# Linear attention and a gated block on one core: operands spaced apart in SBUF, sums of squares by tokens, paired stores, another order of the products

## The chip, the cores and the metric

The kernel runs on one core of a Trainium2 chip. The metric is the time of one execution on the device in microseconds (us); of several runs the median counts. One execution of the kernel before was recorded by the profiler. TensorE is called PE here (its weight loads PEld), VectorE DVE, ScalarE ACT, GpSimd POOL and SyncE SP; SBUF is the memory on the core that the engines read, PSUM the banks that PE writes.

## What is computed

```python
def phi(x):
    proj = np.einsum('bhsd,df->bhsf', x, w_phi)
    proj = proj - np.max(np.abs(proj), axis=-1, keepdims=True)
    return np.concatenate([np.exp(proj), np.exp(-proj)], axis=-1)
q_p, k_p = phi(q), phi(k)
kv, z = np.einsum('bhsf,bhsd->bhfd', k_p, v), np.sum(k_p, axis=2)
attn = np.einsum('bhsf,bhfd->bhsd', q_p, kv) / (np.einsum('bhsf,bhf->bhs', q_p, z)[..., None] + 1e-06)
x = attn.transpose(0, 2, 1, 3).reshape(B * S, H * D)
xn = x / np.sqrt(np.mean(x * x, axis=-1, keepdims=True) + 1e-06) * rms_g
g = xn @ w_gate
out = (g / (1.0 + np.exp(-g)) * (xn @ w_val)) @ w_out
```

All is float32: 8 batches of 8 heads, 576 positions, head size 64, 128 features; then x is 4608 x 512, the gate and the value weights are 512 x 1536, the output weights 1536 x 512.

## The kernel before

A float32 operand of a large product is split into a high and a low part of the type fp32r, and three matmuls (high with high, high with low, low with high) take the place of one. Nearly every matmul has 128x128 weights (the second operand named in a row of the trace) and 256 columns that stream through them (the moving operand, named first). The work goes through four stages, which overlap at their seams.

**Attention** (to about 480 us) runs over 32 pairs of heads (`front`, `mid`, `back`, `last`); lines 339 to 341 are the projections, line 443 the products with kv, the results go to the DRAM tile `xs`, transposed (channels by tokens).

**Fills** (`fill`, line 488) make 3 of the 12 column blocks of gate and value straight: for each of 18 blocks of 256 tokens, 6 units of 12 matmuls (line 503). Six blocks and a half run among the attention's work, 11 and a half behind it, until 608 us. A block is fetched from `xs` on ACT's queue (`load_x`), cast to the high part by ACT and subtracted to the low part by POOL (`_split`, lines 60 and 61), multiplied; ACT copies each unit's 128x256 result from PSUM to a tile `fo` (line 506; six buffers), and one DMA each stores it in `gvs` (line 507; ACT's queue in this stage). While the attention runs a unit takes one of the two PSUM buffers `fp`, and after it one of the three buffers `sm`. With the block's first unit pair goes `total` (line 169): the sums of squares over channels, from two fp32r matmuls with a 128x128 matrix of ones as weights' partner; ACT casts the high part (`sl`, one buffer, the low part by POOL), copies the 128x256 result and stores one row of it in DRAM (`ssd`). `invert` fetches several blocks of them, takes the root and the reciprocal, and stores the result (`rid`), from where `fetch_ri` spreads it over 128 partitions. The x operands of the fills are laid out by `apart`: the first of four channel chunks lies by itself, and the other three 48 floats (192 bytes) further on.

**Gate and value** (608 to about 1060 us) make the other 9 column blocks by a 2x2 scheme with seven products in place of eight, over 9 batches of 512 tokens. A `Group` (line 747) holds two column blocks, or one in the case of `(8,)`; a product is 6 matmuls for each column block (line 763). Products 1, 6, 7 and 4 of a group share one PSUM tile `r1`, each adding to what stands there: after 1 and after 6 ACT copies it (lines 771 and 780), after 7 and after 4 DVE adds or multiplies it in (lines 787, 790). So 6 waits for the copy of 1, 7 for the copy of 6, and 4 for the addition of 7. Products 5 and 3 share `r5` in the same way; Silu follows 3. The order of the products is written out in the loop from line 830: `run(1)` of a group, `run(7)` of the group before, then 5, 2, `run(4)` of the group before, 6, 3. A scheduler with a timeline of its own then merges it with the rest. The x operands of the next batch (`operands_x`, tiles `xo`) are made meanwhile. The results of all 12 column blocks go to the DRAM tile `hs`. In the last batch the groups run in the order `LAST`, and the output weights are fetched (`fetch_o`), combined and split (`split_o`) between groups, two of the six `kp` pieces at a time; the last two pieces, `wh4`/`wl4` and `wh5`/`wl5`, are split behind the last group.

**Output** (to the end) makes 18 groups of 256 tokens, seven products of 18 matmuls each (line 992, `omm`): operands a11, a12, s4, a22, s1, s2, s3 from one load of `hs` (`hload`, SP's queue, two buffers `ht`), split by ACT and POOL one group ahead; here the split weights `wh`, `wl` are the moving operand.

Where the SBUF tiles lie follows from the order of the pools and the sizes in them. Worked out from the program, the moving operand and the weights of a matmul lie at addresses whose difference, modulo 256 bytes, is 0 in all 3402 matmuls of line 763 and all 2268 of line 992; in the fills it is 0 for the first chunk (a quarter of line 503) and 192 for the other three; in the projections 64, and in line 443 either 0 or 128.

```python
nc.tensor.matmul(fp[:, 0:TF], w, at(xx[x], c), start=(i == 0), stop=(i == 3 * NC - 1))      # 503
nc.tensor.matmul(self.r[r][:, k], w[:, cs], x[:, h, c], start=(first and k == 0 and i == 0), # 763
nc.tensor.matmul(place[n], a[:, kp], w[:, o], start=(first and kp == 0 and i == 0),          # 992
LAST = [(8,), (0, 1), (2, 3), (4, 5), (6, 7)]                                                # 825
```

Of the kernel before, what the change touches and what calls it, by code (L numbers as in the profile page):

```python
# [82 lines left out]
def kernel(ctx: ExitStack, tc: tile.TileContext, q, k, v, w_phi,  # L83
# [20 lines left out]
    RW = 5  # L104
# [7 lines left out]
    ssd = dram.tile([1, N], F32, name="ssd")  # L112
# [10 lines left out]
    x_ctx = ExitStack()  # L123
    wfp = x_ctx.enter_context(tc.tile_pool(name="wfp", bufs=1))
# [14 lines left out]
    ones = gl.tile([128, 128], F32R, name="ones")  # L139
    nc.vector.tensor_copy(ones, one.broadcast_to([128, 128]))  # L140
# [9 lines left out]
    def apart(pool, name, n):  # L150
        t = pool.tile([128, 2, NC * n + 64], F32R, name=name)
        return [(t[:, i, 0:n].rearrange("p (c n) -> p c n", c=1), t[:, i, n + 48:n + 48 + (NC - 1) * n].rearrange("p (c n) -> p c n", c=NC - 1))
                for i in range(2)]

    def at(x, c):
        return x[1][:, c - 1] if c else x[0][:, 0]
# [12 lines left out]
    def total(bk, s2, fp, o):  # L169
# [5 lines left out]
    def invert(b0, b1):  # L175
        n = (b1 - b0) * TF // 128
        r = gl.tile([128, n], F32, name=f"inv{b0}")
        cs = slice(b0 * TF, b1 * TF)
        nc.sync.dma_start(out=r, in_=ssd[0, cs].rearrange("(p n) -> p n", p=128))
        nc.scalar.activation(r, r, AF.Sqrt, scale=1.0 / DM, bias=eps)  # L180
        nc.vector.reciprocal(r, r)
        nc.sync.dma_start(out=rid[0, cs].rearrange("(p n) -> p n", p=128), in_=r)
# [31 lines left out]
    a_ctx = ExitStack()  # L214
    xfp = a_ctx.enter_context(tc.tile_pool(name="a_xf", bufs=2))
# [3 lines left out]
    wk = a_ctx.enter_context(tc.tile_pool(name="a_wk", bufs=2))  # L219
    const = a_ctx.enter_context(tc.tile_pool(name="a_const", bufs=1))  # L220
    big = a_ctx.enter_context(tc.tile_pool(name="a_big", bufs=2))
# [6 lines left out]

    ident = const.tile([128, 128], F32, name="ident")
    make_identity(nc, ident)  # L230
# [257 lines left out]
    def fill(bk, xr):  # L488
        xx = dict(zip("hl", apart(xfp, "xo", TF)))
        with late():  # L490
            for k, x in zip(range(2), (xr[:, 0:1], xr[:, 1:NC])):
                _split(nc, xx["h"][k], xx["l"][k], x)
        with late():
            s2 = squares(xr)

        def unit(j, wi):
            js = slice(j * 128, (j + 1) * 128)
            fp = ps_s.tile([128, 512], F32, name="sm") if ended else ps_f.tile([128, T], F32, name="fp")
            i = 0
            for c in range(NC):  # L500
                a, al = wf1[wi][0][:, c, js], wf1[wi][1][:, c, js]
                for w, x in ((a, "h"), (a, "l"), (al, "h")):
                    nc.tensor.matmul(fp[:, 0:TF], w, at(xx[x], c), start=(i == 0), stop=(i == 3 * NC - 1))  # L503
                    i += 1
            o = xfp.tile([128, TF], F32, name="fo", bufs=6)
            nc.scalar.copy(o, fp[:, 0:TF])
            (nc.scalar if tail else nc.sync).dma_start(out=gvv[j][:, wi, bk * TF:(bk + 1) * TF], in_=o)
            if j == 0 and wi:
                fp = ps_s.tile([128, 512], F32, name="sm") if ended else ps_f.tile([128, T], F32, name="fp")
# [555 lines left out]
```

## Time and profile before

| | us |
|---|---|
| median of 3 runs | 1335.52 |
| lowest and highest of them | 1332.21 to 1337.31 |
| the profiled execution, its own time | 1331.64 |
| its span in the profile | 1329.9 |

In that span PE is busy for 1261.0 us (95%), DVE for 976.7 (73%), ACT for 766.3 (58%), POOL for 745.2 (56%); PE runs 10,362 instructions. In the chain of work that ended last PE has 41% of the span, DVE 8% and DMA 6%. A matmul of PE counts as busy until its modelled end, and matmuls overlap: a row with one of them shows 0.28 us, a row of six 0.88, so that five of them take 0.60. The pace is what each further matmul adds. A row of the timeline begins with the start in us and the duration in us; behind the operation stand out and in (moving operand, then weights), partitions, elements and type, and the count; in brackets the idle time ahead of it, and what ended it.

### The profile page before, as it was taken

To read this page: it belongs to the slowest core of one execution; us is meant where nothing else is said; L and a number is where in the kernel's file an instruction comes from. 1 tells how busy PE (TensorE), PEld (TensorE's weight loads), DVE (VectorE), ACT (ScalarE), POOL (GpSimd) and SP (SyncE) were. 2 spreads that over 40 slices of the span, in tenths; PEclk is the share of its full clock that TensorE was granted. 3 is DMA by queue.
4 is the path that set the end of the run, shared out by engine and by line. 5 is a ranking of instruction groups with operands and counts; after the bars stand their busy time and mean duration, and the time that the engine had idled before them with its cause. 6 is when DMAs were issued, how large, how long until landed. Compare 5 with 4: busy or idle time off the path is not lost.

```text
span 1329.9 us, 27502 instructions
## 1 busy us (share of the span) xinstructions
PE 1261.0 (95%) x10362; PEld 1243.1 (93%) x10362; DVE 976.7 (73%) x1410; ACT 766.3 (58%) x1631; POOL 745.2 (56%) x678
## 2 busy tenths in 40 slices
PE   7989999999999987989899999999999699999999
PEld 7989999999999987889899899999999699999998
DVE  6998997988787634654577778786557798877673
ACT  6988888888888755654344444443344333434332
POOL 4766665766655553772334534443332578867773
PEclk9999999999999998999999999999999699999999
DMA  5555666666665245643445554554344445444431
GB/s 160 133 149 160 176 163 171 165 183 190 169 170 148 77 134 161 199 139 108 136 159 175 162 167 159 191 155 158 121 143 136 142 147 155 128 150 153 142 128 49
DMA packets 195209, 199.77 MB, mean 150 GB/s; under 512 B 69042, under 2 KB 148804, under 8 KB 195076
## 3 DMA queue, kind: packets, MB, share of 16 engines
q1 hardware_dynamic: 175184, 179.11, 45.4%
q10 hardware_dynamic: 19892, 18.90, 4.5%
q8 instruction: 82, 1.34, 0.4%
q14 instruction: 51, 0.42, 0.1%
HBM read 128.42 MB, written 69.54 MB: 149 GB/s over the span
## 4 chain that ended last, share of the span: by engine, by line
PE 41%; DVE 8%; DMA 6%; issue 2%; ACT 2%; POOL 1%; ACTq 0%; SPq 0%; DVEq 0%; POOLq 0%
PE r L763 19%; PE gy L992 6%; PE gz L992 6%; PE gd L992 5%; PE fp L992 3%; DMA gvr<-gvs 2%; PE sm L503 2%; DMA x<-xs 1%; DVE x L191 1%; DMA hs<-gvr 1%; DVE gvr L738 1%; DVE wl L61 1%; DMA ht<-hs 1%; DVE stg L55 1%; DVE c L791 1%
## 5 line engine op out<-in xcount | busy, mean ns | idle before, releaser
L763 PE MATMUL r<-xo,wh 128*128 128x256 f32 x1764 | 326.5, 285 | 15.0 <-DVE c L787 8.8
L763 PEld LDWEIGHTS r<-xo,wh 128*128 128x128 f32 x1764 | 276.6, 193 | 18.1 <-DVE c L787 10.1
L408 POOL TENSOR_TENSOR ql<-eq,qh 128x256 fp32r<-128x256 f32 x256 | 216.9, 878 | 59.9 <-ACT qh L404 37.3
L763 PE MATMUL r<-xo,wl 128*128 128x256 f32 x882 | 246.1, 284 | 0.0
L763 PEld LDWEIGHTS r<-xo,wl 128*128 128x128 f32 x882 | 168.9, 193 | 0.0
L343 DVE TENSOR_REDUCE mx<-pp 128x4 f32<-128x512 f32 (+1 forms) x160 | 100.3, 631 | 41.3 <-PE pp L341 40.2
L379 PE MATMUL acc<-vm,ek 128*128 128x65 f32 x1024 | 129.6, 267 | 0.0
L379 PEld LDWEIGHTS acc<-vm,ek 128*128 128x128 f32 x1024 | 126.1, 192 | 0.0
L404 ACT ACTIVATE qh<-sm 128x512 fp32r<-128x512 f32 (+1 forms) x192 | 97.6, 509 | 0.0
L61 POOL TENSOR_TENSOR xo<-x,xo 128x512 fp32r<-128x512 f32 x45 | 65.4, 1463 | 47.9 <-ACT xo L60 47.7
L339 PE MATMUL pp<-wh,th 128*128 128x256 f32 x288 | 88.2, 308 | 2.6 <-DVE yk L346 1.2
L403 ACT ACTIVATE eq<-sm 128x512 f32<-128x512 f32 x128 | 78.7, 615 | 18.8 <-PE sm L392 18.0
L341 PE MATMUL pp<-wh,tl 128*128 128x256 f32 x288 | 84.2, 299 | 0.9 <-DVE tl L61 0.9
L340 PE MATMUL pp<-wl,th 128*128 128x256 f32 x288 | 81.5, 284 | 0.0
L366 ACT ACTIVATE ek<-yk 128x512 f32<-128x512 f32 x128 | 75.6, 654 | 2.4 <-DVE yk L346 2.2
L784 ACT ACTIVATE c<-c 128x1024 f32<-128x1024 f32 (+1 forms) x45 | 43.9, 976 | 53.1 <-DVE c L783 53.1
L780 ACT COPY c<-r 128x512 f32<-128x512 f32 (+1 forms) x45 | 24.4, 543 | 78.8 <-PE r L763 78.7
L61 POOL TENSOR_TENSOR s2l<-st,s2h 128x768 fp32r<-128x768 f32 x18 | 36.6, 2033 | 59.2 <-ACT s2h L60 59.2
L410 POOL TENSOR_TENSOR ql<-eqr,qh 128x256 fp32r<-128x256 f32 x32 | 24.8, 775 | 78.9 <-ACT qh L404 78.9
L54 POOL TENSOR_TENSOR wa<-raw,wa 128x192 f32<-128x192 f32 x64 | 40.8, 658 | 34.6 <-DVE wa L52 18.5
L61 DVE TENSOR_TENSOR tl<-sm,th 128x512 fp32r<-128x512 f32 (+1 forms) x96 | 50.6, 540 | 12.5 <-ACT th L60 12.4
L339 PEld LDWEIGHTS pp<-wh,th 128*128 128x128 f32 x288 | 55.3, 192 | 4.7 <-issue 2.2
(248 smaller groups left out, 4155.9 us busy)
## 6 DMA issues: line engine op xcount, KB each, us to landing
ht<-hs SPq DMA_DIRECT2D x18, 1536.0 KB
hs<-c SPq DMA_DIRECT2D x36, 512.0 KB
gvr<-gvs SPq DMA_DIRECT2D x27, 512.0 KB
rc<-di SPq DMA_DIRECT2D x32, 288.0 KB
x<-xs ACTq DMA_DIRECT2D x18, 512.0 KB
x<-xs SPq DMA_DIRECT2D x9, 1024.0 KB
gvs<-fo ACTq DMA_DIRECT2D x70, 128.0 KB
kt<-in_k_dram SPq DMA_DIRECT2D x32, 256.0 KB
```

The source lines that it names most:

```text
L61: (lo_eng or nc.vector).tensor_tensor(lo, x, hi.bitcast(F32), ALU.subtract)
L339: nc.tensor.matmul(o, th[:, cs], wh, start=True, stop=False)
L340: nc.tensor.matmul(o, th[:, cs], wl, start=False, stop=False)
L341: nc.tensor.matmul(o, tl[:, cs], wh, start=False, stop=True)
L343: nc.vector.tensor_reduce(mx[:, 0:2 * m], pp[:, 0:2 * m], axis=AX.X, op=ALU.max, apply_absolute_value=True)
L366: nc.scalar.activation(e[h][:, sg], y["k", h], AF.Exp, scale=1.0 - 2.0 * sg)
L379: nc.tensor.matmul(acc[:, sg, h], e[h][:, sg, j], vm[:, h, j], start=False, stop=(h == 1 and j == T0 - 1))
L403: nc.scalar.activation(ei[:, sg], yi, AF.Exp, scale=1.0 - 2.0 * sg)
L404: nc.scalar.activation(hi[:, sg], yi, AF.Exp, scale=1.0 - 2.0 * sg)
L408: nc.gpsimd.tensor_tensor(lo[:, sg, cs], ei[:, sg, cs], hi[:, sg, cs].bitcast(F32), ALU.subtract)
L763: nc.tensor.matmul(self.r[r][:, k], w[:, cs], x[:, h, c], start=(first and k == 0 and i == 0), stop=(i == 3 * NP1 - 1), skip_group_check=True)
L992: nc.tensor.matmul(place[n], a[:, kp], w[:, o], start=(first and kp == 0 and i == 0), stop=(kp == KP - 1 and i == 2), skip_group_check=True)
```

## The change

- Pads (`LPAD`, `FPAD`, `GPAD`, `OPAD`, `CPAD`, `BPAD`: unused tiles of 8 to 48 floats) shift the tiles behind them. Worked out as above, the difference modulo 256 bytes is 192 in all matmuls of gate, output and fill (lines 767, 999 and 497 of the new kernel) and in the projections, and 64 or 192 in the products with kv. `apart` is gone: the x operands of a fill are one tile, cast by one instruction in place of two.
- Sums of squares: the low and high parts are gone. `total` takes the squares themselves as weights, in two plain float32 matmuls with one column of ones each, so that the sums land by tokens, 128 partitions x 2; ACT copies those into the SBUF tile `sums`. `invert` works there, transposes the result by PE and DVE, and stores it. `ssd` and its DMAs are gone; `sl` has two buffers.
- Stores: gate and value of a column block share a tile `fo`, and one DMA stores both: 54 in place of 108. After the attention the units take `sm` and `fp` in turn (`bank`), five PSUM buffers in place of three.
- Order: product 7 of a group is written behind 3 of the same group. `LAST` begins with `(0, 1)` and ends with `(8,), (6, 7)`; `last_o` fetches, combines and splits output weights from the first group on. The first `ht` is fetched by two DMAs of half the size from ACT's queue.

```diff
@@ squares, total, invert
-        s2 = xm.tile([128, 2, TF], F32R, name="sl", bufs=1)
-        nc.gpsimd.tensor_tensor(ss[:, 0:TF], ss[:, 0:TF], ss[:, TF:T], ALU.add)
-        _split(nc, s2[:, 0], s2[:, 1], ss[:, 0:TF], lo_eng=nc.gpsimd)
+        s2 = xm.tile([128, TF], F32, name="sl", bufs=2)
+        nc.gpsimd.tensor_tensor(s2, ss[:, 0:TF], ss[:, TF:T], ALU.add)
...
-        for i in range(2):
-            nc.tensor.matmul(fp, ones, s2[:, i], start=(i == 0), stop=(i == 1))
-        nc.scalar.copy(o, fp)
-        nc.scalar.dma_start(out=ssd[:, bk * TF:(bk + 1) * TF], in_=o[0:1])
+        for i in range(TF // 128):
+            nc.tensor.matmul(fp[:, i:i + 1], s2[:, i * 128:(i + 1) * 128], one, start=True, stop=True)
+        n = TF // 128
+        nc.scalar.copy(sums[:, bk * n:(bk + 1) * n], fp[:, 0:n])
@@ fill
-        xx = dict(zip("hl", apart(xfp, "xo", TF)))
+        xx = dict(zip("hl", (xfp.tile([128, NC, TF], F32R, name="xo" + n) for n in "hl")))
...
-            fp = ps_s.tile([128, 512], F32, name="sm") if ended else ps_f.tile([128, T], F32, name="fp")
+            fp = bank()
...
-            o = xfp.tile([128, TF], F32, name="fo", bufs=6)
-            nc.scalar.copy(o, fp[:, 0:TF])
-            (nc.scalar if tail else nc.sync).dma_start(out=gvv[j][:, wi, bk * TF:(bk + 1) * TF], in_=o)
+            if not wi:
+                o[j] = xfp.tile([128, 2, TF], F32, name="fo", bufs=3)
+            nc.scalar.copy(o[j][:, wi], fp[:, 0:TF])
+            if wi:
+                (nc.scalar if tail else nc.sync).dma_start(out=gvv[j][:, :, bk * TF:(bk + 1) * TF], in_=o[j])
@@ the gate loop
-    LAST = [(8,), (0, 1), (2, 3), (4, 5), (6, 7)]
+    LAST = [(0, 1), (2, 3), (4, 5), (8,), (6, 7)]
...
-            if prev:
-                prev.run(7)
             gr.run(5)
...
-            if last and n == 0:
-                wot = [fetch_o(0), fetch_o(1)]
-            if last and n > 1:
...
+            if last:
+                last_o(n)
...
+            gr.run(7)
             prev = gr
@@ hload
-        nc.sync.dma_start(out=h, in_=hsv[:, :, gi * 256:(gi + 1) * 256])
+        if gi == 0:
+            for r in range(2):
+                nc.scalar.dma_start(out=h[:, r::2], in_=hsv[:, r::2, 0:256])
+        else:
+            nc.sync.dma_start(out=h, in_=hsv[:, :, gi * 256:(gi + 1) * 256])
```

How instructions stand one behind another on an engine shows at three places. The first is ACT in the fill stage, around one block: `sl` are the squares that are split, `fo` the results of units, `x` a block as fetched, `xo` its operands. Before:

```order
L506 COPY fo_8351<-sm_8338 128x256
L60 CAST sl_8331<-ss_8329 128x256
L507 DMA gvs_58<-fo_8351 128x256
L60 CAST xo_8453<-x_8440 128x256
L60 CAST xo_8453<-x_8440 128x768
L163 ACTIVATE sq_8459<-x_8440 128x512
L506 COPY fo_8367<-sm_8354 128x256
L163 ACTIVATE ss_8458<-x_8440 128x512
L172 COPY fo_8371<-sm_8370 128x256
L506 COPY fo_8389<-sm_8376 128x256
L507 DMA gvs_58<-fo_8367 128x256
```

In the kernel after, at a like place (`xoh` is the high part of `xo`):

```order
L501 COPY fo_8409<-fp_8396 128x256
L155 ACTIVATE ss_8591<-x_8574 128x512
L155 ACTIVATE sq_8592<-x_8574 128x512
L501 COPY fo_8409<-sm_8411 128x256
L501 COPY fo_8439<-fp_8426 128x256
L503 DMA gvs_58<-fo_8409 128x2x256
L501 COPY fo_8439<-sm_8441 128x256
L60 CAST xoh_8587<-x_8574 128x1024
L503 DMA gvs_58<-fo_8439 128x2x256
```

The cast of `sl` and the store behind each copy are gone; one store stands behind two copies, which come from `sm` and `fp` in turn.

The second is PE around the sums of one block, among fill matmuls (`fg`, `fv` are fill weights, `one` the column of ones). Before:

```order
L503 MATMUL sm_9010<-xo_8980,fv1_79 128x256
L171 MATMUL sm_9026<-sl_8987,ones_93 128x256
L763 MATMUL r2_9526<-xo2_8977,wl3_8220 128x256
L171 MATMUL sm_9026<-sl_8987,ones_93 128x256
L503 MATMUL sm_9032<-xo_8980,fg0_76 128x256 x2
L503 MATMUL sm_9032<-xo_8980,fg1_77 128x256
```

After:

```order
L497 MATMUL sm_8731<-xoh_8705,fv1_79 128x256
L497 MATMUL sm_8731<-xoh_8705,fv0_78 128x256
L497 MATMUL sm_8731<-xol_8706,fv0_78 128x256
L497 MATMUL sm_8731<-xoh_8705,fv1_79 128x256
L163 MATMUL fp_8746<-one_86,sl_8714 128x1 x2
L497 MATMUL sm_8750<-xoh_8705,fg0_76 128x256
L497 MATMUL sm_8750<-xol_8706,fg0_76 128x256
```

Two matmuls of 256 columns have become two of one column each, whose weights are the squares.

The third is ACT behind the last products of the gate stage: `r1` is the PSUM tile of products 1, 6, 7 and 4, `wh4` and `wh5` the last two pieces of the output weights, `ht` the first load for the output stage, `a11h` and `s3h` its operands. Before:

```order
L771 COPY c1_14093<-r1_14095 128x2x256
L784 ACTIVATE c1_13975<-c1_13975 128x1024
L60 CAST wh3_8219<-x_13934 128x1024
L780 COPY c1_14093<-r1_14095 128x2x256
L60 CAST wh4_8221<-stg0_8231 128x768
L784 ACTIVATE c1_14093<-c1_14093 128x1024
L60 CAST wh4_8221<-stg1_8232 128x1024
L60 CAST wh5_8223<-x_14056 128x768
L60 CAST wh5_8223<-x_14056 128x1024
L60 CAST a11h_14267<-ht_14263 128x768
```

After:

```order
L775 COPY c1_13946<-r1_13948 128x2x256
L784 COPY c1_13946<-r1_13948 128x2x256
L60 CAST wh4_8128<-stg1_8139 128x1024
L788 ACTIVATE c1_13946<-c1_13946 128x1024
L60 CAST wh5_8130<-x_13821 128x768
L968 DMA ht_14094<-hs_59 128x6x256 x2
L60 CAST wh5_8130<-x_13821 128x1024
L60 CAST a11h_14099<-ht_14094 128x768
L60 CAST a12h_14103<-ht_14094 128x768
L60 CAST s3h_14116<-st_14107 128x768
```

Of the four casts behind the last copy two, those of `wh5`, stand behind Silu now, and the loads of `ht`, which ACT now issues itself, stand between them.

## Rows read from the trace of the kernel before

**Rows 1.** Stages: window, length, busy PE, PEld, DVE, ACT, POOL (instructions), granted clock, DMA, GB/s.

```profile
480.00:608.00 128.00, 108.80 (x875) 104.55 (x874) 59.00 (x72) 68.43 (x161) 65.44 (x50) 0.97 0.53 164
608.00:1010.00 402.00, 390.36 (x3208) 387.14 (x3208) 286.25 (x414) 176.96 (x318) 163.46 (x142) 1.00 0.47 152
1010.00:1060.00 50.00, 36.44 (x240) 34.71 (x239) 37.51 (x46) 22.53 (x31) 19.40 (x9) 0.76 0.51 162
1060.00:1330.00 270.00, 265.02 (x2206) 264.61 (x2205) 200.47 (x174) 101.18 (x134) 192.55 (x88) 1.00 0.42 129
```

**Rows 2.** PE and PEld busy in line 763, in 992, in 992 mid-stage; clock, DMA, GB/s.

```profile
0.00:1330.00 1330.00, 418.39 (x3402) 413.85 (x3402) 0.99 0.50 150
0.00:1330.00 1330.00, 276.92 (x2268) 275.69 (x2268) 0.99 0.50 150
1100.00:1300.00 200.00, 200.00 (x1669) 200.00 (x1669) 1.00 0.45 138
```

**Rows 3.** Timeline of PE in the gate stage: start, us, what, count.

```profile
641.22 0.88 PE L763 MATMUL r<-xo,fg 128*128 128x256 f32 x6
641.94 0.88 PE L763 MATMUL r<-xo,fv 128*128 128x256 f32 x6
```

**Rows 4.** Timeline of PE in the fill stage.

```profile
565.43 0.85 PE L503 MATMUL sm<-xo,fg 128*128 128x256 f32 x6
566.34 1.54 PE L503 MATMUL sm<-xo,fv 128*128 128x256 f32 x12
```

**Rows 5.** Timeline of PE, a fill among attention work.

```profile
360.19 0.87 PE L503 MATMUL fp<-xo,fv 128*128 128x256 f32 x6
```

**Rows 6.** Timeline of PE in attention, products of lines 339 to 341 and 443.

```profile
361.73 0.28 PE L339 MATMUL pp<-wh,th 128*128 128x256 f32 x1
...
362.08 0.29 PE L443 MATMUL sm<-qh,kv1h 128*65 128x288 f32 x1
...
363.39 0.29 PE L443 MATMUL sm<-ql,kv1h 128*65 128x288 f32 x1
```

**Rows 7.** Timeline of PE, a plain f32 product (two records) and the next two.

```profile
363.65 0.39 PE L374 MATMUL acc<-vr,er 128*128 128x130 f32 x2
363.79 0.36 PE L339 MATMUL pp<-wh,th 128*128 128x256 f32 x1
363.99 0.28 PE L340 MATMUL pp<-wl,th 128*128 128x256 f32 x1
```

**Rows 8.** Waits of PE in the fill stage, 480 to 608: us, count, longest.

```profile
PE sm L503 <- ACT fo L506: 6.0, 6, 1.7
PE sm L503 <- ACT xo L60: 4.2, 1, 4.2
```

**Rows 9.** Timeline of ACT, and below it the chain, in the fill stage.

```profile
508.25 0.41 ACT L60 CAST sl<-ss 128x256 fp32r<-128x256 f32 x1 [1.81 <-POOL ss L165]
...
532.35 5.82 DMA x<-xs
```

**Rows 10.** Waits of PE, 608 to 1010 us, and a group of ACT instructions.

```profile
PE r L763 <- DVE c L790: 6.0, 6, 1.4
PE r L763 <- DVE c L787: 5.0, 4, 2.4
...
L780 ACT COPY c<-r 128x512 f32<-128x512 f32 x36 | 21.1, 585 | 65.9 <-PE r L763 65.9
```

**Rows 11.** End of the gate stage: waits of PE, chain, window.

```profile
PE fp L992 <- ACT a11h L60: 5.5, 2, 4.7
PE r L763 <- DVE c L787: 3.8, 2, 3.7
...
1017.33 5.53 DMA x<-wos
...
1036.37 7.52 DMA ht<-hs
...
1044.00:1052.00 8.00, 4.58 (x18) 3.99 (x18) 3.65 (x4) 1.03 (x2) 2.28 (x1) 0.50 0.67 224
```

More of the change, by code (lines that the diff above doesn't have):

```diff
@@ L111 @@
     wos = dram.tile([128, KP, 4, DH], F32, name="wos")
-    ssd = dram.tile([1, N], F32, name="ssd")
     rid = dram.tile([1, N], F32, name="rid")
@@ L123 @@
     x_ctx = ExitStack()
+    gl.tile([128, LPAD], F32, name="lpad")
     wfp = x_ctx.enter_context(tc.tile_pool(name="wfp", bufs=1))
@@ L138 @@
     nc.scalar.activation(warm, one, AF.Exp)
-    ones = gl.tile([128, 128], F32R, name="ones")
-    nc.vector.tensor_copy(ones, one.broadcast_to([128, 128]))
+    ident = gl.tile([128, 128], F32, name="ident")
+    make_identity(nc, ident)
+    sums = gl.tile([128, N // 128], F32, name="sums")
     held = []
@@ L148, in fetch @@
         return x
[L150 to L156, printed above, removed]
     def squares(x):
@@ L214 @@
     a_ctx = ExitStack()
+    a_ctx.enter_context(tc.tile_pool(name="fpad", bufs=1)).tile([128, FPAD], F32, name="fpad")
     xfp = a_ctx.enter_context(tc.tile_pool(name="a_xf", bufs=2))
@@ L502, in unit, with bank @@
                 for w, x in ((a, "h"), (a, "l"), (al, "h")):
-                    nc.tensor.matmul(fp[:, 0:TF], w, at(xx[x], c), start=(i == 0), stop=(i == 3 * NC - 1))
+                    nc.tensor.matmul(fp[:, 0:TF], w, xx[x][:, c], start=(i == 0), stop=(i == 3 * NC - 1))
                     i += 1
-            o = xfp.tile([128, TF], F32, name="fo", bufs=6)
-            nc.scalar.copy(o, fp[:, 0:TF])
-            (nc.scalar if tail else nc.sync).dma_start(out=gvv[j][:, wi, bk * TF:(bk + 1) * TF], in_=o)
+            if not wi:
[3 more added lines that the diff above has]
+                (nc.scalar if tail else nc.sync).dma_start(out=gvv[j][:, :, bk * TF:(bk + 1) * TF], in_=o[j])
             if j == 0 and wi:
-                fp = ps_s.tile([128, 512], F32, name="sm") if ended else ps_f.tile([128, T], F32, name="fp")
-                total(bk, s2, fp[:, 0:TF], xfp.tile([128, TF], F32, name="fo", bufs=6))
+                total(bk, s2, bank())
                 summed.append(bk)
         return [lambda j=j, wi=wi: unit(j, wi) for j in range(J1) for wi in range(2)]
+    banks = [0]
+    def bank():
+        banks[0] += 1
+        if ended and banks[0] % 2:
+            return ps_s.tile([128, 512], F32, name="sm")
+        return ps_f.tile([128, T], F32, name="fp")
     PR = B * NP
@@ L592 @@
     stg = [wtp.tile([128, 1024], F32, name=f"stg{i}") for i in range(2)]
+    g_ctx.enter_context(tc.tile_pool(name="gpad", bufs=1, side="right")).tile([128, GPAD], F32, name="gpad")
     xops = [g_ctx.enter_context(tc.tile_pool(name="xop0", bufs=1, reuse_waits="tile", side="right"))]
@@ L823, with last_o @@
     GROUPS = [(0, 1), (2, 3), (4, 5), (6, 7), (8,)]
-    LAST = [(8,), (0, 1), (2, 3), (4, 5), (6, 7)]
+    LAST = [(0, 1), (2, 3), (4, 5), (8,), (6, 7)]
+    def last_o(n):
+        nonlocal wot
+        if 0 < n <= KP // 2:
+            with late():
+                for o in wot:
+                    combine_o(*o)
+            with late():
+                for o in wot:
+                    split_o(*o)
+        wot = [fetch_o(kp) for kp in (2 * n, 2 * n + 1) if kp < KP]
     assert not todo
@@ L849 @@
                 prev.run(4)
-            if last and n == 0:
-                wot = [fetch_o(0), fetch_o(1)]
-            if last and n > 1:
-                with late():
-                    for o in wot:
-                        split_o(*o)
-                    wot = [fetch_o(kp) for kp in (2 * n - 2, 2 * n - 1) if kp < KP]
-                    for o in wot:
-                        combine_o(*o)
+            if last:
+                last_o(n)
             gr.run(6)
@@ L885 @@
                 decs.pop(0)()
-            if last and n == 1:
-                with late():
-                    for o in wot:
-                        combine_o(*o)
         if not last:
             xb, ri = xbn, rin
-    prev.run(7)
     prev.run(4)
@@ L901, in left @@
         return ctx.enter_context(tc.tile_pool(name=name, bufs=bufs, reuse_waits="tile"))
+    left("opad").tile([128, OPAD], F32, name="opad")
     ohps = [left("ohp1"), left("ohp0")][::-1]
```

28 lines of the change are left out of this document (15 added, 13 removed).

## The prediction

> **What bounds the kernel now.** I read the table of stages first [rows 1]: in the gate stage (608 to 1010 us) PE is busy for 390.4 of 402 us, in the output stage (1060 to 1330) for 265.0 of 270. DVE reaches at most 74% there, POOL 71%, ACT 44%, the DMAs 47%. In these 672 us the time is the number of matmuls by the pace of one, and a faster helper is worth little. The two other stretches are different: behind the attention (480 to 608) PE idles for 19.2 of 128 us, at the seam (1010 to 1060) for 13.6 of 50, with the granted clock down to a mean of 0.76.
>
> So the second look is at the pace. Two groups of six gate matmuls start 0.72 us apart: 120 ns each [rows 3]. In the output stage 1669 fill 200 us: 119.8 [rows 2]. Matmuls of the same shape and types in the fill stage go faster: a row of six lasts 0.85 us, a row of twelve 1.54, and a single one 0.28 [rows 6], so each further one takes (0.85 - 0.28) / 5 = 114 or (1.54 - 0.28) / 11 = 114.5 ns [rows 4]. The clock does not explain it: it was 1.00 in the slower stage and 0.97 in the faster one [rows 1]. Nor does the name of the weights: rows 3 and 4 both have `fg` and `fv` there. What differs by the program is where the moving operand lies against the weights: 0 mod 256 bytes in gate and output, 192 in three chunks of four in the fills. The evidence is not clean, since the same fill among the attention's work goes at (0.87 - 0.28) / 5 = 118 [rows 5], and three projections, at 64, take 0.35 us or 117 each [rows 6]. I take spacing as the cause, and 118 as a second pace that a stretch may fall into.
>
> The third look is at the waits, named below where a part touches them.
>
> **The change part by part**, against the profiled execution's 1331.6 us.
>
> A. *Pace of gate and output.* All 3402 + 2268 = 5670 matmuls [rows 2] move from 0 to 192. At the fills' 114 ns: 5670 x 6 = 34 us. Not all of it arrives: waits for ACT, DVE and DMA don't shrink, and a PE that is ahead meets them sooner; the gate stage has 11.6 us of them [rows 1], of which I let a quarter grow back, 3 us. **-31**. Ends: at 117.5, between the slower rows of 192 and of 64 [rows 5, 6], 5670 x 2.5 = 14; at 113.5, which the rounding of the row of twelve allows [rows 4], 36. Below that nothing in the trace goes with 256 columns.
>
> B. *Fill matmuls and sums.* A quarter of the 1296 fill matmuls moves from 0 to 192: 324 x 6 ns = -2. The sums lose 36 matmuls at some 118 ns, 4.2 us, and gain 36 plain float32 products. The trace has one such product: its two records take 0.14 us, and the matmul behind the next starts 0.20 us later where 0.12 is usual [rows 7]. Ends: 36 x 0.14 = 5.0, or +0.8; with the slow successor as well, 36 x 0.22 = 7.9, or +3.7, and somewhat more if a one-column product waits for its weights. I take +2, and **0** for B.
>
> C. *Attention.* The 864 projections move from 64 to 192, the 768 products with kv from 0 or 128 to 64 or 192. These take (363.39 - 362.08) / 10 = 131 ns for 288 columns [rows 6]; at the fills' pace 288 / 256 x 114 = 128. That is 864 x 3 + 768 x 3 ns = 5 us if PE alone set this stage. **-3**, ends -5 and 0.
>
> D. *Waits of the fill stage.* PE waits six times for a copy `fo` by ACT, 6.0 us, at most 1.7 each, and once 4.2 us for the cast `xo` [rows 8]. ACT works in order: the cast of `sl` stood 1.81 us for POOL's sum [rows 9], and the copies that free PSUM stand behind it. The change takes that cast away, halves the stores that ACT issues, and adds two PSUM buffers, two units of 12 x 0.114 = 1.4 us, more than the longest of these waits. So I take all of the 6.0 and, since a fetch can still be late, half of the 4.2: **-8**. What is late next is the block's own cycle: a fetch of 5.8 us [rows 9], a cast of 1024 and two squares of 512 floats at the 585 ns per 512 of a copy [rows 10], some 8.2 us, against 72 x 0.114 + 0.45 for sums and seams = 8.7 on PE (the 0.45 an estimate from rows 7). That is nearly even, so the ends are wide: 0 if the fetches set the stage, -19 if all idle time goes. One thing speaks against it: gate matmuls stood between fills before and filled some gaps; now the first of them follows the last fill.
>
> E. *The seam.* [...] The weights now come a group earlier, and two casts fewer stand ahead of a11h. On the other hand products 6, 7 and 4 of the last group follow each other with nothing between, so 7 waits for ACT's copy and 4 for DVE's addition, about 2.5 us; and ACT issues the loads of `ht` only behind Silu and a cast, while the second load goes out on SP without waiting and shares the DMAs with them. SP is spared the first load, and ACT's two casts behind it wait for no one else. Ends -6 (half of what the seam loses) and +6 (a load that takes half as long again, 4 us, and what a slower clock adds). **0**.
>
> F. *Order in the gate stage.* Product 7 now follows 3 of its own group. Waits for the additions of 7 and 4 were 5.0 and 6.0 us in 402 [rows 10]; the new order has a wait for the copy in place of some. Ends -6 and +10; **0**. The fetches and combining of output weights start a group earlier on SP, DVE and POOL, which have room [rows 1].
>
> Sum: -31 + 0 - 3 - 8 + 0 + 0 = **-42**: 1289.6 for the profiled execution. That lay 3.9 us below the median of the runs, 1335.5, by which it would be 1293.5. I take 1291.
>
> [...] By rows 3 and 4 equal matmuls differ by 6 ns. [...]
>
> **The rivals.**
>
> *The slower pace at 192.* Gate and output settle at 117.5 ns as the fill among attention did [rows 5]: A is -14 less the same 3 or so, B and C are near 0, D stays. 1331.6 - 13 - 8 = about 1310 (1308 without the reserve). For it: rows 5 and 6. Against: the two rows of the fill stage, whose neighbours, like those of the gate stage, are matmuls of 256 columns.
>
> *Spacing changes nothing.* The fills may be faster by something else, such as shorter runs. Then A and C are 0, D stays: 1331.6 - 8, about 1322 with a little more for sums and order. This is also the case in which the change doesn't do what it says. Against: rows of six in both stages, 0.88 against 0.85 [rows 3, 4].
>
> *Slower: product 7 waits for ACT in every group.* 7 adds to the tile that ACT copies after 6. With nothing but product 3 between, the cover is 12 x 0.12 = 1.44 us, or 0.72 for `(8,)`. The last matmul's tail of 0.28 and the copy of 0.585 [rows 10] fit in; a Silu of 1024 floats on ACT ahead of it (some 1.1 us, estimated from two such copies) doesn't, by 0.5 us, nor does (8,)'s. If that happens in all 45 groups, 36 x 0.5 + 9 x 1.2 = 29 us are lost; at the worst, 45 x 1.35 = 61. It decides from about 1 us per group, where it eats all 42: the time would be 1350. Against: the copy of 6 stands ahead of the Silu of its own group, and ACT is busy for 44% there [rows 1].
>
> *Everything comes in.* 113.5 ns, a fill stage with hardly a gap (-15) and a seam that gains 6: 1331.6 - 36 - 3 - 15 - 6 = about 1270.
>
> **How the numbers follow.** The forecast has 0.67, the slower pace 0.15, no effect of spacing 0.08, slower 0.03, everything 0.07. From the ends of the forecast's own terms (A 14 to 36, D 0 to 19, E and F some 6 each, not all at one end) its own range is about 1277 to 1305. Range: to keep no more than 2 in 10 outside I reach to the slower pace and to the good end, **1272 to 1309**. Half a per cent is 6.7 us, about what a measurement of this kernel can tell from no change: faster by more than that 0.93 (all but the third rival and half of the second), within it 0.04, slower by more 0.03.
>
> **What would show it.** Right: rows of six gate matmuls of 0.85 us, 200 us of output work with some 1750 matmuls in place of 1669, a fill stage without waits for `fo` over 1 us, and PE idle there well under 19 us. Wrong: rows of six still at 0.88; waits of gate matmuls for the copy of line 784 (new numbering) with a count near 45; a wait for a11h of over 8 us or a longer stretch at 0.50; a fill stage as long as before, waiting for `x`.

## The result and the profile after

| | before | changed |
|---|---|---|
| median of the runs, us | 1334.83 (4 runs) | 1321.56 (4 runs) |
| lowest and highest | 1332.21 to 1337.31 | 1318.34 to 1323.44 |
| span of the record | 1329.9 | 1321.6 |

The ratio is 0.990, with an interval of 0.987 to 0.993: the kernel gains 1.0%, 13 us, where 1291 (44 us off the median then known) had been forecast. The time lies outside the stated range, above its upper end of 1309.

The pace came in. The page of windows (window, length, busy PE with its count, PEld, clock, DMA, GB/s), first all matmuls of gate (line 767) and output (line 999), then the output's in 200 us, to set beside [rows 2]:

```profile
0.00:1321.00 1321.00, 403.48 (x3402) 399.38 (x3402) 0.98 0.50 151
0.00:1321.00 1321.00, 263.12 (x2268) 261.67 (x2268) 0.98 0.50 151
1100.00:1300.00 200.00, 200.00 (x1767) 200.00 (x1766) 1.00 0.47 145
```

In 200 us stand 1767 matmuls, 113.2 ns each, where 1669 stood before (119.8). The gate has this pace too, in some stretches; in others it runs at another one. Gate matmuls of the changed kernel in two windows without a wait:

```profile
716.00:736.00 20.00, 20.00 (x179) 20.00 (x178) 1.00 0.52 172
...
910.00:940.00 30.00, 30.00 (x257) 30.00 (x256) 1.00 0.39 132
```

That is 112 and 117 ns, at the same addresses (a short window also counts matmuls that only reach into it). By the starts of all matmuls between the 378th and the 3024th of the gate (seven of its nine batches), 1320 follow at 113 or 114 ns and 1098 at 115 to 118, here called 117 (140 more at 119).

Where the gain went shows in the table by stage (columns as in [rows 1]):

```profile
480.00:608.00 128.00, 109.47 (x872) 105.90 (x871) 54.77 (x67) 65.05 (x146) 61.68 (x45) 0.95 0.53 163
608.00:1010.00 402.00, 383.06 (x3245) 380.35 (x3244) 266.52 (x403) 173.19 (x317) 162.77 (x141) 0.98 0.46 150
1010.00:1060.00 50.00, 32.79 (x242) 30.62 (x241) 38.77 (x58) 24.83 (x34) 21.02 (x8) 0.85 0.58 190
1060.00:1321.00 261.00, 256.86 (x2244) 255.99 (x2243) 200.98 (x176) 97.26 (x136) 195.55 (x89) 1.00 0.43 134
```

In the gate stage PE is idle for 18.9 us of 402 (11.6 before), and its mean clock is 0.98 in place of 1.00. The same windows hold nearly the same number of matmuls as before: 3245 against 3208. Two marks and the end cut the span: the last start in the row of products with kv that is shown, and the first start of an output matmul. The page of single lines, of before and of after (name, count, least, median and largest ns, first and last start):

```profile
L443 PE MATMUL sm<-qh,kv0h x80: 290/294/378, 187.1 to 471.7; 128*65 128x288 f32 x80
...
L992 PE MATMUL fp<-wh,a11h x108: 279/283/580, 1045.1 to 1313.2; 128*128 128x256 f32 x108
```

```profile
L437 PE MATMUL sm<-qh,kv0h x80: 289/293/380, 191.0 to 477.6; 128*65 128x288 f32 x80
...
L999 PE MATMUL fp<-wh,a11h x108: 276/276/579, 1052.2 to 1305.6; 128*128 128x256 f32 x108
```

| part of the span | before | after | difference | forecast |
|---|---|---|---|---|
| attention, to the first mark | 471.7 | 477.6 | +5.9 | -3 |
| fills, gate, seam, to the second | 573.4 | 574.6 | +1.2 | -25 |
| output, to the end | 284.8 | 269.4 | -15.4 | -14 |

(The forecast's 31 us for gate and output are shared out by count: 2268 x 6 ns for the output, the rest, with the 8 us of the fill stage, to the middle.) The output stage did what was forecast. The middle, where 25 us should have gone, gained nothing, and the attention lost 6. The two records lie 8.3 us apart and the medians 13.3; the record of the changed kernel is of the slowest of its four runs, 1323.44.

What PE waited for in the gate stage (608 to 1010 us: total, times, longest), for [rows 10]:

```profile
PE r L767 <- DVE c L794: 13.8, 6, 4.0
PE r L767 <- DVE c L781: 3.2, 3, 1.7
PE r L767 <- ACT c L775: 1.5, 1, 1.5
```

Line 794 is DVE's multiplication behind product 4 (790 before), which sets free the tile `r1`. The longest of the six, on PE, on DVE ahead of it, and on SP:

```profile
704.93 1.65 PE L767 MATMUL r<-xo,fv 128*128 128x256 f32 x6 [3.98 <-DVE c L794]
```

```profile
701.66 1.23 DVE L742 TENSOR_TENSOR gvr<-gvr,ri 128x1024 f32<-128x1024 f32 x1 [3.07 <-DMA gvr<-gvs]
...
703.00 0.68 DVE L787 TENSOR_TENSOR c<-c,r 128x512 f32<-128x512 f32 x1
703.60 0.68 DVE L744 TENSOR_TENSOR gvr<-gvr 128x512 f32<-128x512 f32 x1
704.20 0.68 DVE L794 TENSOR_TENSOR c<-c,r 128x512 f32<-128x512 f32 x1
```

```profile
693.93 0.38 SPq L745 DMA_DIRECT2D hs<-gvr  x1
694.36 0.42 SPq L261 DMA_DIRECT2D wos<-stg  x1
697.95 0.37 SPq L738 DMA_DIRECT2D gvr<-gvs  x1
```

`gvr` has one buffer. The product of gate and value leaves it for `hs` at 693.9; the next load, ahead of which SP waited 3.1 us for that store, is issued at 698.0 and lands at 701.7. DVE, whose rows follow the program's order, stands at line 742 until then; the multiplication of line 794 is queued behind it, and PE behind that. Of the six waits for line 794, four (11.6 of the 13.8 us) follow such a stand of DVE at line 742; the other two stand behind other work of DVE. Then PE runs at half the clock for a while, by the windows around it:

```profile
690.00:704.00 14.00, 10.95 (x97) 10.75 (x95) 9.30 (x14) 6.01 (x12) 3.83 (x6) 1.00 0.39 126
704.00:712.00 8.00, 7.07 (x37) 7.07 (x38) 6.72 (x11) 2.34 (x6) 5.71 (x6) 0.57 0.71 243
712.00:740.00 28.00, 28.00 (x249) 28.00 (x248) 17.62 (x30) 12.01 (x23) 10.20 (x10) 1.00 0.47 156
```

37 matmuls in the 7.1 us from 704.9 on, most of them at half the clock (0.50 from 705 to 710 us, 0.57 on the mean of the window), and 249 in the next 28. At 113 ns the 37 would have taken 4.2 us, so the wait of 4.0 us cost some 7.

### The profile page after: what moved, and what is told of

It reads as the page before. It is cut to its first block, busy times and chain, and to the rows that moved or that the text cites. A ratio compares the mean times of both kernels' runs of the same rounds, so it can differ in the third digit from the quotient of the medians.

```text
span 1321.6 us, 27396 instructions
## 1 busy us (share of the span) xinstructions
PE 1242.5 (94%) x10401; PEld 1223.8 (93%) x10401; DVE 951.3 (72%) x1394; ACT 747.3 (57%) x1595; POOL 731.9 (55%) x660
## 5 line engine op out<-in xcount | busy, mean ns | idle before, releaser
L767 PE MATMUL r<-xo,wh 128*128 128x256 f32 x1764 | 312.2, 280 | 7.9 <-DVE c L794 4.1
L767 PEld LDWEIGHTS r<-xo,wh 128*128 128x128 f32 x1764 | 268.9, 190 | 10.1 <-DVE c L794 4.7
L767 PE MATMUL r<-xo,wl 128*128 128x256 f32 x882 | 242.1, 279 | 0.0
L61 POOL TENSOR_TENSOR xo<-x,xo 128x512 fp32r<-128x512 f32 x45 | 60.7, 1355 | 41.5 <-ACT xo L60 41.5
L497 PE MATMUL fp<-xoh,fg 128*128 128x256 f32 x336 | 72.9, 293 | 5.1 <-ACT xoh L60 3.7
L61 POOL TENSOR_TENSOR s2l<-st,s2h 128x768 fp32r<-128x768 f32 x18 | 42.3, 2352 | 49.5 <-ACT s2h L60 42.9
L497 PE MATMUL fp<-xoh,fv 128*128 128x256 f32 x320 | 65.9, 285 | 3.9 <-ACT fo L501 3.3
L54 POOL TENSOR_TENSOR stg<-stg,stg 128x128 f32<-128x128 f32 x48 | 23.8, 518 | 80.7 <-DVE stg L52 48.3
L767 PE MATMUL r<-xo,fv 128*128 128x256 f32 x324 | 49.7, 287 | 16.5 <-DVE c L794 12.4
L61 POOL TENSOR_TENSOR wl<-stg,wh 128x1024 fp32r<-128x1024 f32 x10 | 24.5, 2452 | 72.5 <-ACT wh L60 72.5
```

The lines of the kernel that those rows point to most:

```text
L61: (lo_eng or nc.vector).tensor_tensor(lo, x, hi.bitcast(F32), ALU.subtract)
L497: nc.tensor.matmul(fp[:, 0:TF], w, xx[x][:, c], start=(i == 0), stop=(i == 3 * NC - 1))
```

## The experiments

Theory 1: the pace is set by the distance, and in the gate stage the round trip of `gvr` through DMA takes its gain back. Theory 2: the new order of the products makes the waits. Times of experiments are medians; each experiment ran beside the kernel before on the same chip. What is said of stages comes from one record of each.

**The spacing alone.** The kernel before with pads, so that gate, fill and output are at 192 (which also makes the operands of a fill one tile, cast by one instruction, as in the changed kernel):

```diff
+    FPAD, GPAD, OPAD = 48, 16, 16
...
-        xx = dict(zip("hl", apart(xfp, "xo", TF)))
+        xx = dict(zip("hl", (xfp.tile([128, NC, TF], F32R, name="xo" + n) for n in "hl")))
+    g_ctx.enter_context(tc.tile_pool(name="gpad", bufs=1, side="right")).tile([128, GPAD], F32, name="gpad")
+    left("opad").tile([128, OPAD], F32, name="opad")
```

> The kernel before with nothing but unused tiles that put the moving operand 192 bytes (mod 256) from the weights in all gate, fill and output matmuls; order, sums, stores and loads as before. Theory 1 (the pace of one matmul comes in as forecast, 120 to 113-115 ns, and in the gate stage a fixed round trip through DMA, the load of gvr that stands in DVE's order ahead of the additions PE waits for, takes most of it back): output stage 266 us in place of 281, gate stage shorter by only 5 to 12, whole about 1310. Theory 2 (the round trip is harmless, the new order of the products made the waits): with the old order the gate stage gains its full 20 us too, whole about 1297. If spacing were not the cause of the pace: 1335.

Measured: 1320.6 against 1335.3, ratio 0.990 (0.987 to 0.993). So the pads alone give as much as the whole change; the rest of it, taken together, gave nothing (which hides a loss and a gain, see the old order below). In the output 1767 matmuls stand in 200 us, as in the changed kernel. In the gate stage the pace was there, at its faster value:

```profile
900.00:980.00 80.00, 80.00 (x706) 80.00 (x707) 1.00 0.44 144
```

113.3 ns; and yet the matmuls 378 to 3024 of the gate took 321.3 us (before: 327.2), since waits of over 0.28 us rose from 8.0 to 14.5 and matmuls at half clock from 15 to 52. Theory 2 alone, with 1297, falls: the old order loses the gain as well. The measured time is some 10 us above theory 1 too: from the end of the attention to the 378th gate matmul the record has 185.9 us, 178.2 before. Why is open.

**Everything but the spacing of gate and output.** The changed kernel without `gpad` and `opad`.

> The changed kernel without the two pads of gate and output, so that these 5670 matmuls are at 0 mod 256 again. Theory 1: output stage 281 again (+15.5), gate matmuls at 120 ns but fewer waits, gate stage longer by 5 to 10; whole 1342 to 1347, above the kernel before. Theory 2: the waits stay, since the order makes them, and gate and output lose all of it: +35, about 1356.

Measured: 1339.4, ratio 1.0031 (1.0018 to 1.0044); the output has 1669 matmuls in 200 us again. The change without these two pads costs 4 us, and the two pads are worth 18 here. Theory 1 is the nearer one, though 1339 lies below its 1342; theory 2's 35 us is refuted.

**The load of gvr set free.** In the changed kernel the product of gate and value goes to its own tile, for which `c2` gives up its third buffer:

```diff
-            self.c2 = ev.tile([128, 2, HT], F32, name="c2")[:, 0:self.m]
+            self.c2 = ev.tile([128, 2, HT], F32, name="c2", bufs=2)[:, 0:self.m]
...
-        nc.vector.tensor_tensor(r[:, 0], r[:, 0], r[:, 1], ALU.mult)
-        nc.sync.dma_start(out=hsv[:, j, bk * T:(bk + 1) * T], in_=r[:, 0])
+        o = rwp.tile([128, T], F32, name="gvo")
+        nc.vector.tensor_tensor(o, r[:, 0], r[:, 1], ALU.mult)
+        nc.sync.dma_start(out=hsv[:, j, bk * T:(bk + 1) * T], in_=o)
```

> The changed kernel, in which the product of gate and value goes to a tile of its own (gvo; c2 gives up its third buffer for it), so that the next load of gvr need not wait until the store has left. Theory 1: DVE's waits for the gvr load fall from 15 to under 6 us between 660 and 990, PE's waits in the gate stage from 18.5 to about 10, and its clock drops less; whole 1308 to 1314 in place of 1321.6. Theory 2: PE's waits stay, whole within 4 us of 1321.6.

Measured: 1298.9, ratio 0.9725 (0.970 to 0.975), 23 us under the changed kernel, more than expected. In the gate stage (608 to 1010 us) DVE's wait for the load in the changed kernel; then, with the edit, PE's wait for the same multiplication (13.8 us above) and DVE's for the load:

```profile
DVE gvr L742 <- DMA gvr<-gvs: 19.2, 8, 4.3
```

```profile
PE r L768 <- DVE c L795: 4.1, 5, 1.8
...
DVE gvr L742 <- DMA gvr<-gvs: 9.8, 9, 2.4
```

DVE's wait is halved and not gone; between 660 and 990 us it fell from 14.9 to 7.4, where under 6 was expected.

**The old order of the products.** In the changed kernel, `run(7)` of a group stands behind `run(1)` of the next again.

```diff
             gr.run(1)
+            if prev:
+                prev.run(7)
...
-            gr.run(7)
             prev = gr
```

> The changed kernel with product 7 of a group back behind product 1 of the next group. Theory 1: gate stage within 4 us, whole 1317 to 1326, and DVE's waits for gvr still over 10 us. Theory 2: PE's waits for the additions fall to about the 11 us of before, whole about 1311.

Measured: 1304.5, ratio 0.977 (0.975 to 0.979): 17 us under the changed kernel, more than theory 2 had asked for (1311). Neither theory had both. The waits for line 794 fell to 7.2 us, and DVE's for the load from 19.2 to 12.7:

```profile
PE r L767 <- DVE c L794: 7.2, 6, 2.2
```

The pads alone have the old order too, and took 1320.6. So with this order the other parts of the change (sums, stores, PSUM buffers, last batch, pads of the attention) are worth 16 us together, about what the new order costs; which of them, no run shows.

**Both.** The two edits together, to see whether they remove one wait or two.

> The changed kernel with both edits that helped alone: product 7 behind product 1 of the next group, and the product of gate and value in a tile of its own. If they remove the same wait (PE waiting for additions queued behind a load of gvr on DVE): little more than the better of the two, 1296 to 1300, gate stage about 316 us from its 378th to its 3024th matmul. If they remove different waits: the gains of 17 and 23 add in part, gate stage near 2646 x 0.1135 = 300 to 308 us, whole 1284 to 1292.

Measured: 1301.5 (ratio 0.9732, 0.971 to 0.976): no better than the freed load alone (1298.9; the intervals overlap). By the times this looks like one wait, which the order lengthens and the load causes. The waits themselves don't show that: PE's in the gate stage (608 to 1010 us) add up to 18.9 us in the changed kernel, 10.6 with the load free, 14.2 with the old order and 3.9 with both, so there the two edits add. But in the record of both most gate matmuls kept the slower pace, 117 ns (1912 of those between the 378th and the 3024th, 1000 with the load free), which costs some 4 us more:

```profile
900.00:970.00 70.00, 70.00 (x597) 70.00 (x596) 1.00 0.44 144
```

**The freed load in the kernel before, with and without spacing.**

> The kernel before with only two edits: the pads of e1_pads_only, and the gate-value product in a tile of its own as in e3_gvr_result_apart. If the load of gvr is what took the gain of the pace back, in the old order too: PE's waits in the gate stage fall, its 2646 matmuls take 303 to 310 us (321 with the pads alone), whole 1300 to 1308. If in the old order it was something else: within 4 us of the 1320.6 of the pads alone.

> The kernel before with the gate-value product in a tile of its own, and no pads: gate matmuls at 120 ns. If the round trip binds only at the faster pace: its 8 us of waits between the 378th and the 3024th gate matmul can at most go, whole 1328 to 1334 against 1335 to 1337. If the edit helps for a reason of its own, whatever the pace: 1312 to 1318, as far below as in the changed kernel.

Measured: 1303.2 with the pads (ratio 0.976, 0.972 to 0.980), 1320.3 without (0.989, 0.987 to 0.991). So the edit is worth some 15 us in the kernel before already, at 120 ns a matmul; my condition that the load binds only at the faster pace is refuted. With the load free, the pads are worth 17 us. The edit gives 15 us before, 17 with the pads, 23 in the changed kernel. Not all of that is PE's wait in the gate stage: without pads those waits fell from 11.6 to 3.1 us. The edit also spares SP's queue its stand for the store of `gvr` (41.9 us of 402 before, 40.6 in the changed kernel, none with the edit): in the changed kernel's rows of SP above nothing is issued between 694.8 and 698.0 us. The runs don't part the two.

**Distances.** The changed kernel with the gate at 64 and the output at 128.

> The changed kernel with the gate operands 64 and the output operands 128 apart (mod 256) in place of 192. If any distance but 0 will do: output group of 126 matmuls 14.3 us as at 192, gate matmuls at 113 to 117 ns. If 128 is as bad as 0: 15.1 us for each group of the output.

Measured, one run: 1332.4. The output holds 1688 matmuls in 200 us, 118.5 ns, nearer to 0 than to 192. Of the gate's 2646 matmuls 2242 follow at about 117 ns, and 69 at 113; but in its first batch there is a stretch at 113 (179 matmuls from 616 to 636 us, as many as at 192 in the window above). So not any distance will do: 0 went at 120 and 128 at 118.5, while 64 and 192 both had 113 and 117, and one record doesn't tell them apart.

**The seam.** The first load of `ht` on SP again:

> The changed kernel with the first load of ht by SP in one DMA again, ahead of the second. In the changed kernel the gap between the last gate and the first output matmul was 10.5 us (5.2 before): ACT issued the load behind a cast that waited for the last weights, after SP's second load. If that is the cause: gap 4 to 6 us, whole 1315 to 1318. If the order of the last batch is (7 and 4 of the last group with nothing between): gap still 9 to 11, whole 1319 to 1324.

Measured: 1322.2 (ratio 0.989, 0.987 to 0.991), no gain. The gap between the last gate and the first output matmul was 7.8 us. In the record of the changed kernel it was 10.5, where ACT issued the load at 1043.0 behind a cast that waited for weights:

```profile
1042.98 0.83 ACT L60 CAST wh<-x 128x768 fp32r<-128x768 f32 x1 [1.85 <-DMA x<-wos]
1042.99 1.10 ACTq L968 DMA_DIRECT2D ht<-hs  x2
1046.59 1.04 ACT L60 CAST wh<-x 128x1024 fp32r<-128x1024 f32 x1 [2.77 <-DVE x L815]
1051.32 0.83 ACT L60 CAST a11h<-ht 128x768 fp32r<-128x768 f32 x1 [3.69 <-DMA ht<-hs]
```

but 6.2 in its second record (below), and 3.3 and 1.8 with the freed load and with the old order. It lies between the two expectations, and the whole time gained nothing, so the queue is not what sets it. I read it as following how the gate stage ends; no run tests that.

**The fill stage.** PE waited there for other things than before (total, times, longest; 480 to 600 us of the changed kernel):

```profile
PE fp L497 <- DVE xol L61: 6.5, 2, 6.0
PE fp L497 <- ACT fo L501: 4.2, 6, 1.5
PE fp L497 <- ACT xoh L60: 3.7, 1, 3.7
```

Before the 6.0 us DVE stood 4.5 us for `ri` and then worked 5.85 us on the first gate operand, with the fill's subtraction behind it. The next kernel, on top of the freed load, gives that subtraction to POOL:

```diff
-            _split(nc, xx["h"], xx["l"], xr)
+            _split(nc, xx["h"], xx["l"], xr, lo_eng=nc.gpsimd if ended else None)
```

> The kernel of e3_gvr_result_apart, in which POOL and not DVE subtracts the low part of a fill's operand once the attention has ended. In the changed kernel PE waited 6.0 us there for DVE, which had waited 4.5 us for ri and then worked 5.9 us on the first gate operand. If that is why the fill stage gained nothing: fill stage 120 us in place of 125 to 127, whole 1292 to 1295. If the fetches of x set that stage, or POOL is as late: fill stage within 2 us, whole 1297 to 1301 or above.

Measured: 1303.7 (ratio 0.977, 0.974 to 0.980), against 1298.9 without the edit: nothing gained. From the last product with kv to the last fill matmul, its record has 130.7 us against 125.1. The wait went, and others came in its place:

```profile
PE fp L173 <- DVE sums L171: 4.7, 1, 4.7
PE fp L497 <- ACT xoh L60: 3.7, 1, 3.7
PE fp L497 <- ACT fo L501: 3.1, 4, 1.0
PE fp L497 <- POOL xol L61: 3.0, 1, 3.0
```

**The attention.** First its addresses: the changed kernel without `cpad` and `bpad`, so that projections and products with kv lie as before.

> The changed kernel without the two pads of the attention, so that projections (64) and products with kv (0 or 128) lie as before; gate, fill and output stay at 192. The attention ended at 486.8 us with the change and at 480.1 before. If the new addresses cost that: end at 480 to 482, whole about 1316. If the sums, or the other order in which fills fall among the attention's work, cost it: end at 485 to 488, whole 1318 to 1324.

Measured: 1320.1 (ratio 0.988, 0.986 to 0.991); the last of all products with kv starts at 488.1 us (480.1 in the record of before, 486.8 in that of the changed kernel), so the addresses are not it. Then the sums alone in the kernel before:

> The kernel before with the new sums of squares alone (squares as weights, one column, no split, no DRAM round trip, roots worked out on chip); all gate and output operands at 0 as before. Forecast of this term: +2 us on PE, and waits of the fill stage down by some 6, so 1329 to 1333 against 1335. If the sums cost the attention its 6 us: its end at 485 or later, and the whole at 1337 to 1342.

Measured: 1338.3, ratio 1.0012 (1.0001 to 1.0024): a loss of 1.4 us where a gain of 2 to 6 was forecast, and the attention ends at 485.3, which is the second case of the expectation. (1.4 us of the 5 is fill work: 12 fill matmuls more stand ahead of that mark.) Then a second record of each kernel:

> The changed kernel once more, for a second record of its stages. If the 6.7 us that the attention lost in the first record, and the fill stage that gained nothing, belong to the change: attention ends at 484 to 489 us again, and the fill stage takes 125 to 129. If they were chance of one execution: attention ends at 480 to 482, or the fill stage takes 120 to 123. Whole about 1321 either way.

> The kernel before once more, for a second record of its stages: attention ends at 480 to 481 and the fill stage takes 128 if the first record was typical; 484 or later, or a fill stage that differs by over 3 us, would put the loss of the attention down to chance. Whole about 1335.

Measured: 1323.9 and, one run, 1332.8; the attention ended at 490.5 and at 479.0 us, the fill stage (from there to the last fill matmul) took 124.6 and 129.9; in the first pair it was 127.1 and 128.1. The loss in the attention belongs to the change. In this pair it is 11.5 us, and from there to the first output matmul 8.7 are gained. Last the old sums in the changed kernel, alone and with the freed load:

> The changed kernel with the old sums of squares (split, two matmuls with ones, round trip through DRAM), all distances of gate, fill, output and projections at 192 as in the change. The attention ended at 486.8 and 490.5 us in two records of the change, at 480.1 and 479.0 before, and at 485.3 with the new sums alone. If the sums cost it: end at 480 to 483, whole 1315 to 1318. If the other edits of the fills (one cast, paired stores) do: end at 486 or later, whole 1320 to 1324.

> The same with the gate-value product in a tile of its own. If the two losses are separate, the sums in the attention and the load of gvr in the gate stage: 1292 to 1296, below the 1298.9 of that tile with the new sums. If the sums cost nothing: 1298 to 1302.

Measured: 1319.0 (ratio 0.987, 0.984 to 0.990) and 1297.8 (0.973, 0.971 to 0.975); the attention ends at 482.4 and 482.2. By the records the sums cost the attention some 5 us: in all eleven records with the new sums the last product with kv starts at 484.2 to 490.5 us, in all seven with the old ones at 479.0 to 483.3. By the medians the old ones are 3 us better in the changed kernel and 1 us with the freed load, within the intervals. The products show their own price at most blocks: in the changed kernel four records in a row, and the next two fill matmuls:

```profile
547.56 0.28 PE L497 MATMUL fp<-xoh,fv 128*128 128x256 f32 x1
547.68 0.50 PE L163 MATMUL sm<-one,sl 128*128 128x1 f32 x4
548.04 0.36 PE L497 MATMUL fp<-xoh,fg 128*128 128x256 f32 x1
548.24 0.28 PE L497 MATMUL fp<-xol,fg 128*128 128x256 f32 x1
```

0.36 us for the four, and 0.20 to the matmul after the next: 0.56 for a block, against 3 x 0.118 for the old two with the matmul behind them, +0.2, or 3.7 us for 18 such blocks. About 1.3 of that lies in the attention. Part of the rest lies near 280 us, where PE waits for DVE: the granted clock falls there in nine of the eleven records with the new sums, and in one of the seven with the old. With the new sums alone:

```profile
270.00:280.00 10.00, 7.15 (x61) 6.75 (x59) 7.54 (x14) 7.92 (x20) 5.17 (x7) 1.00 0.37 95
280.00:290.00 10.00, 10.00 (x73) 10.00 (x72) 5.65 (x11) 6.66 (x18) 2.81 (x4) 0.83 0.97 259
```

Before, the second window had 88 matmuls at 1.00. The two records with new sums and no such fall still end at 484.9 and 484.4, so this is not all of it; what makes the wait longer stays open.

## Why the prediction was wrong

**A, the pace: half right.** In the output it came in whole: 113.2 ns, -15.4 us by the marks. The gate was to give 20 us less a reserve of 3 for waits that grow. Between its matmuls 378 and 3024 it gave none: 327.2 us before, 329.5 after (329.2 and 326.7 in the second records). Of the 17.5 us that 2646 matmuls at 113.4 ns would save, waits of over 0.28 us took 8.8 (8.0 to 16.8), matmuls at half clock 4.8 (52 more by 0.092), and the slower pace of 1098 matmuls 4.5: 18.1 of the 19.8 us that are missing. The last had been given a chance as a rival, but for all of gate and output, and it came in stretches of the gate. (That rival was also added up wrongly: -14 and a reserve of 3 make -11, so about 1313 and not 1310. A range that reached there would have missed as well.) The step that failed is the reserve of 3 us: I took a quarter of 11.6 us, and did not ask what DVE itself waited for. In its place the runs showed waits, half clock and slower pace that took back all of the gate's gain; with the load of `gvr` set free the same matmuls took 316.2 us, and the kernel 23 us less. DVE's waits for that load, and the one buffer of `gvr`, could be read in the trace of before (608 to 1010 us):

```profile
DVE gvr L738 <- DMA gvr<-gvs: 8.4, 7, 3.4
```

**F, the order: the term that was mis-sized.** It stood at 0, with ends of -6 and +10. The old order in the changed kernel is 17 us faster, so the term was +17, beyond its upper end. It is not a second loss beside that of A: with the load free it is gone. The rival put beside it had the right place and the wrong wait: product 7 waiting for ACT's copy of 6 is not among the waits of the gate stage in the changed kernel's record. What it waits for is the tile of an earlier group, held by DVE, most often behind the load of `gvr`. With the load free, the new order costs nothing in time: 1298.9 with it, 1301.5 without.

**B, the sums: 0 was forecast, made of -2 for the fills and +2 for the sums.** The product's price was at the upper end (+3.7, as the slow successor had it), and the attention ends later with the new sums. In the whole time they cost 1.4 us by their own run, 3 by the old ones put back, the latter within the intervals.

**C, the attention: -3 was forecast, +5.9 read.** The addresses gave nothing that shows: by their starts the products with kv follow at 131.8 ns before and 131.5 after, and the projections, now at 192, at 117.5 where they had 117.7 at 64. The sums' 5 us stand against it.

**D, the waits of the fill stage: -8 was forecast, -1 read in the first pair of records and -5 in the second.** PE's idle time from 480 to 608 us stayed, 19.2 us before and 18.5 after. PE's waits for `fo`, 6.0 us with a unit in `sm` and 4.0 with one in `fp`, which the sum had left out, fell to 4.2, as the step wanted, but DVE's subtraction came late in their place. That is nearer to the end of 0 than to the forecast; the next edit there, too, only exchanged one wait for another. Which of the chain of fetch, cast and subtraction sets it has not been settled.

**E, the seam: 0 was forecast.** The gap grew by 5 us in one record and by 1 in the other, within its ends, of which the upper one was worked out from the load of `ht`, 7.52 us before [rows 11].

**The rivals.** That spacing changes nothing is refuted (18 us with the rest of the change, 15 alone, 17 with the load free). With the pads alone the output went from 119.8 to 113.2 ns. The time came out at what the second rival had said, 1322, by another way: the pace was there, and was given back.

The best two, the changed kernel with the freed load (1298.9) and the same with the old sums (1297.8), beat both kernels and can't be told apart.

## What to carry to other kernels

A faster pace is worth its count only where nothing else sets the time: before counting it, follow each wait of the fast engine one engine further, to what the helper was waiting for, and look for a tile with one buffer that is stored and loaded again. Here DVE, whose rows follow the program's order, passed its wait of 3.07 us for the load of `gvr` on to PE as one of 3.98, and that one cost some 7, with the clock at 0.50 after it. What two edits gain alone need not add: 17 and 23 us came to 20 together.

## What the runs showed of the hardware

- Matmuls of 256 columns went at a pace that changed with the distance of the moving operand from the weights, here worked out from the program, modulo 256 bytes: 119.8 ns at 0 (output, before, 1669 in 200 us), 118.5 at 128 (output, `f3_spacings`, one run, 1688), 113.2 at 192 (output, changed and `e1_pads_only`, 1767). The pad of the gate moves the moving operand and that of the output the weights, and both changed the pace. Whether 256 is the right modulus was not tested.
- At 192 two paces were seen at the same addresses, 113 and 117 ns (113.3 on the mean of the stretch from 712 to 739 us of the changed kernel's gate, 117.8 on that from 743 to 789), and so at 64 (gate, `f3_spacings`, one run). In the changed kernel's record a stretch of the gate kept one for up to 102 us (the slower from 883 to 986), and it changed mostly at a wait. In the output the slower one was seen at the start alone (72 and 163 of 2268 matmuls in the two records of the changed kernel). The projections of the attention, at 192 too, followed at 117.5 on the mean. What chooses is open.
- The wait of 4.0 us in the gate of the changed kernel ended at 704.9 us. The granted clock was 0.57 from 704 to 712 us and 0.50 from 705 to 710, and the first six matmuls took 1.65 us, where six took 0.84 at 700.0.
